# Bits of q placed right behind their signs and those of k behind its low rows; the overflow loop ahead of the last expert's closing step

## The chip, the cores and the metric

The kernel runs on one core of a Trainium2 chip. The metric is the time of the whole program on the device, in microseconds (us), as a median over runs. PE is the matrix engine (PEld its weight loads), DVE, ACT and POOL are the vector, scalar and GpSimd engines, and SP is the engine whose queue issues most of the DMA transfers.

## The reference, cut to what matters

Three steps follow each other. The first is attention in which a query sees only keys of its own hash bucket; the other two are feed-forward layers, the last with eight experts.

```python
def _attn_ref(q, k, v, proj):            # 2 batches, 8 heads, 768 rows, 64 columns
    q_bits = (np.einsum('bhsd,dk->bhsk', q, proj) > 0)      # 6 bits a row
    k_bits = (np.einsum('bhsd,dk->bhsk', k, proj) > 0)
    mask = q_bucket[:, :, :, None] == k_bucket[:, :, None, :]
    scores = np.where(mask, scale * np.matmul(q, k.transpose(0, 1, 3, 2)), -1e9)
    ...                                   # softmax, times v
x = _moe_ref(x)                           # 1536 tokens, gated layer 512 -> 1536 -> 512
def _moe2_ref(x, w_skip, w_gate, w1, w2): # 8 experts, tokens with skip_score > 0 only
    for e in range(E):                    # every chosen token goes to its best expert
        h = np.maximum(xc[mask] @ w1[e], 0.0)
        y[mask] = gate_w[mask, None] * (h @ w2[e])
    out[do_compute] = xc + y
```

## The kernel before

**Attention.** Two heads make a pair; there are 8 pairs of 12 units, a unit being 128 query rows of one head. For a unit PE multiplies twice into the same bank (`qk`): `t1q` by `t1k` (L501, 128 rows of operand), then `t2q` by `t2k` (L503, 76 rows: 64 rows of data and 12 rows of bits). Rows 64 to 76 of the t2 operands hold the bits of q and of k with such signs and sizes that products of unlike buckets fall far below the others. DVE takes the peak (L516), ACT the exponential (L530), POOL divides (L522 to L525), PE transposes (L539), and PE multiplies by v (L560).

While pair p-1 is computed, `prep(p)` makes the operands of pair p in the other half of the tile `RG`. Its steps: `cast` (ACT, L449) rounds k and q of one head to the short float type; `low` (DVE, L456) makes what the rounding left, over all 128 partitions of operand 3, so it also writes the rows where the bits of k will lie; `q_rows` (two DMAs, L460) copies q's rounded rows to operands 0 and 1; `k_rows` (one DMA, L463) copies k's within operand 2, over the rows that `q_rows` reads; `ql_rows` (one DMA, L466) copies q's low rows out of operand 3; `bits` (PE, L475) and `signs` (DVE, L478) make the bits in one tile; `place` (eight DMAs, L485) carries them to their rows: for each of two heads and two halves of the sequence one DMA for q (c = 0, operand 1) and one for k (c = 1, operand 3, over rows that `ql_rows` reads). A DMA row `RG<-RG 64x2x768` is 384 KB, one of `place` (`12x384`) 18 KB.

Where a step stands is set by the table `PLAN`: each step has a number in thousandths of a unit, all steps of attention are sorted by it (`at`, and the last lines of `attention`), and each engine takes its instructions in that order. SP's queue is in order: an instruction that waits holds up all behind it. Besides the copies above it carries for each pair the load of k and q of pair p+2 (`load`, L383, 768 KB), the load of v (L391), and on the way two pieces of the next layer's weights of 512 KB (`cv_load`, L226: `SS<-in_wg`, `in_wv`, `in_wo`), which POOL takes first (`cv_rebias`, L229).

**The end.** In `moe2` each expert ends with `deliver` (PE, the second product, L1118 to L1122) and `finish` (DVE, L1126, then a scatter to `out` that POOL issues, L1037). Experts with over 128 tokens are served by a loop behind all this (`over_tile` under `tc.For_i`, L1295 to L1298). Its count `n` is zero with these inputs; every engine still reads `n` (L1296) and takes the way around the body (L1297): it posts its semaphore for the skipped body once its own work is done, POOL waits for all scatters and posts theirs (`INC_SWDGE_SEM`), then every engine waits through a list of 12 semaphore waits, among them those on the scatters and on PE, and goes on to the program's end (L1386), where all engines meet twice.

Of the kernel before, what the change touches and what calls it, by code (L numbers as in the profile page):

```python
# [35 lines left out]
    "low0": 3769,  # L36
    "cast1": 444,
    "low1": 4884,
    "q_rows": 4912,
    "k_rows": 5120,  # L40
    "ql_rows": 6549,
    "place": 9379,
    "load": 16702,
    "bits": 1375,
    "signs": 1759,
# [12 lines left out]
    "first": (585, 787),  # L58
    "others": (2972, 1965, 2133, 3661),
    "warms": ((787, 3), (2467, 3), (2734, 3)),  # L60
}


# [4 lines left out]
def tile_kernel(  # L68
# [17 lines left out]
    nc = tc.nc  # L86
    NPAIR, D2, _, S = kq.shape
# [32 lines left out]
    def f32(ap):  # L120
        return ap.bitcast(F32)
# [252 lines left out]
    def bt_t(p):  # L374
        return rg(16 * S, S)
# [56 lines left out]
    def prep(p):  # L432

        def both(kind, rows):
            o = (p % 2) * 8 * S + kind * S
            return f32(RG[rows, o : o + 8 * S].rearrange("p (j x) -> p j x", j=2)[:, :, 0:S])

        up, dn = slice(0, D), slice(D, 2 * D)  # L440

        def cast(j):
            if PLAN["low"][j] == "P":
                PTS(raw_kq(p, j), raw_kq(p, j), kqs, 1.0, ALU.mult, ALU.mult)
                COPY[PLAN["cast"][j]](out=t_op(p, j, 2), in_=raw_kq(p, j))
            elif PLAN["cast"][j] == "V":
                TS(t_op(p, j, 2), raw_kq(p, j), kqs, None, ALU.mult)
            else:
                nc.scalar.mul(t_op(p, j, 2), raw_kq(p, j), kqs)  # L449

        def low(j):
            o = rg((p % 2) * 8 * S + (j * 4 + 3) * S, S)
            if PLAN["low"][j] == "P":
                PTT(out=o, in0=raw_kq(p, j), in1=f32(t_op(p, j, 2)), op=ALU.subtract)
            else:
                STT(out=o, in0=raw_kq(p, j), scalar=kqs, in1=f32(t_op(p, j, 2)), op0=ALU.mult, op1=ALU.subtract)  # L456

        def q_rows():
            for kind in (0, 1):
                dma(out=both(kind, up), in_=both(2, dn))  # L460

        def k_rows():
            dma(out=both(2, dn), in_=both(2, up))  # L463

        def ql_rows():
            dma(out=both(0, dn), in_=both(3, dn))  # L466

        st = {}

        def bits():  # L470

            st["b"] = psH()
            for t in range(4):
                j, h = divmod(t, 2)
                mm(st["b"][32 * t : 32 * t + 32, 0:HS], lhsT=padg, rhs=raw_kq(p, j)[:, h * HS : (h + 1) * HS], start=True, stop=True)  # L475

        def signs():
            TS(bt_t(p)[:, 0:HS], st["b"][:, 0:HS], thr[:, 0:1], thr[:, 1:2], ALU.is_gt, ALU.mult)  # L478

        def place():  # L480
            for t in range(4):
                j, h = divmod(t, 2)
                for c in range(2):
                    o = 32 * t + 16 * c
                    dma(out=f32(t_op(p, j, 1 + 2 * c)[D:T2R, h * HS : (h + 1) * HS]), in_=f32(bt_t(p)[o : o + 2 * NB, 0:HS]))  # L485

        return cast, low, q_rows, k_rows, ql_rows, bits, signs, place

# [169 lines left out]
    def attention():  # L658
        start_up()
        for u in range(NU):  # L660
            for name, f in (("qk", qk), ("exp", expo), ("tr", back), ("stats", stats)):
                at(1000 * u + PLAN[name][u % 4], f, u)
            for hf in range(2):
                at(1000 * u + PLAN["copy"][u % 4][hf], emptied, u, hf)
        for u in range(0, NU, 2):
            at(1000 * u + PLAN["scales"][u // 2 % 2], scales, u)
        for g in range(NU // 4):
            av_steps(g)
        for p in range(1, NPAIR):
            cast, low, q_rows, k_rows, ql_rows, bits, signs, place = prep(p)  # L670
            o = (p - 1) * PER * 1000 + (PLAN["late"] if p == 1 else 0)

            def put(name, f, *a):
                at(o + PLAN[name], f, *a)

            for j in range(2):
                put(f"cast{j}", cast, j)
                put(f"low{j}", low, j)
            put("q_rows", q_rows)
            put("k_rows", k_rows)  # L680
            put("ql_rows", ql_rows)
            put("bits", bits)
            put("signs", signs)
            put("place", place)
            if p + 2 < NPAIR:
                put("load", load, p + 2)
            at((p - 1) * PER * 1000 + PLAN["v"], load_v, p)
        for x in range(12):
            for y, f in enumerate((cv_load, cv_rebias, cv_shift, cv_low, cv_sign)):
                at(max(6000 * x + PLAN["cv"][y], PLAN["others"][2] + 1), f, x)  # L690
        for x in range(12, 15):
            at(1000 * (NU - 9) + 500, cv_load, x)
        xn = xnorm(0)
        sq, ad, me, fl, sp_, dg, sd, sc, hi_, lo_ = PLAN["xn"]
        for x in range(2):
            at(sq[x], xn["square"], x)
        for x in range(3):
            at(ad[x], xn["add"], x)
        at(me, lambda: xn["mean"](psH()))
        at(fl, xn["flat"])  # L700
        at(sp_, xn["spill"])
        for z in range(2 * TPB):
            at(dg[z // 2], xn["diag"], z)
        at(sd, lambda: xn["spread"](psH()))
        for k in range(NK):
            at(sc[k], xn["scale"], k)
            at(hi_[k], xn["high"], k)
            at(lo_[k], xn["low"], k)
        for x_, f, *a in PLAN["splits"]:
            at(1000 * NU + x_, split_gv if f else split_o, *a)  # L710
        for x_, z in PLAN["ahead"]:
            at(1000 * NU + x_, gate_products, 0, 0, z)
        for _, _, f, a in sorted(cal, key=lambda z: z[:2]):
            f(*a)
# [414 lines left out]
    def moe2(rt):  # L1129
        spl = {}  # L1130
        done = [0]
        state = {}
        over = iter(())

        def prep():
            n = done[0]
            if n < len(SEQ):
                spl[SEQ[n]] = split2(n, wch[n % 9])
                fetch(n + 9)
            done[0] += 1  # L1140
            if n > 6:
                next(over, None)

        for n in range(2):
            spl[SEQ[n]] = early.pop(n)
            done[0] += 1
        r = rt["finish"]()
        over = over_tables(r, state)
        xgs = [xyt[e // TPB][:, e % TPB] for e in range(NE)]
        for e in range(NE):  # L1150
            gather(xgs[e], r["idx"][:, e : e + 1])
            if e == 2:

                for n in range(6, 11):
                    nc.gpsimd.memset(wch[n % 9][0:1, 0, 0:1], 0.0)
                    fetch(n)
        r["rest"]()
        xo = {0: x_ops(0, xgs[0], True)}
        pu = {0: psA()}
        hs = {}  # L1160
        up(pu[0], xo[0], spl.pop((0, 0)), 0)
        prep()
        xo[1] = x_ops(1, xgs[1])
        prep()
        up(pu[0], xo[0], spl.pop((0, 1)), 1)
        hs[0] = relu(0, pu[0])
        r["rest_pe"]()
        prep()
        for e in range(NE):
            nx = e + 1 if e + 1 < NE else None  # L1170
            if nx:
                pu[nx] = psA()
                up(pu[nx], xo[nx], spl.pop((nx, 0)), 0)
            ht = turn(hs.pop(e))
            if nx:
                prep()
                up(pu[nx], xo[nx], spl.pop((nx, 1)), 1)
                hs[nx] = relu(nx, pu[nx])
                prep()
                if nx + 1 < NE:  # L1180
                    xo[nx + 1] = x_ops(nx + 1, xgs[nx + 1])
            ps = bank(6 + e % 2)
            for hf in range(2):
                deliver(ps, ht, spl.pop((e, 2 + hf)), hf)
                if hf:
                    finish(e, ps, xgs[e], r["gate"][:, e : e + 1], r["idx"][:, e : e + 1])
                prep()
        for _ in over:
            pass
        return r, state  # L1190


    def over_tables(r, state):
# [46 lines left out]
    def over_tile(op_, r, o):  # L1240
        cur = op_.tile([P, NTT], F32, name="cur")
        TS(cur, o["j"].broadcast_to([P, NTT]), -float(P), None, ALU.mult)
        TT(out=cur, in0=cur, in1=o["place"], op=ALU.add)
        slots = bank(7)
        for i in range(NTT):
            on = rg(14336 + (i % 2) * P, P)
            TS(on, iot, cur[:, i : i + 1], None, ALU.is_equal)
# [39 lines left out]
            deliver(ps, ht, split2(hf, spl[2 + hf]), hf)  # L1287
        finish(0, ps, xg, gt[:, 0:1], idx[:, 0:1])

    with tc.manual_schedule():  # L1290
        rt = routing()
        attention()
        moe1(rt)
        r, o = moe2(rt)
        with tc.tile_pool(name="op", bufs=1) as op_:  # L1295
            n = nc.values_load(o["n"][0:1, 0:1], min_val=0, max_val=NTT - 1)  # L1296
            with tc.For_i(0, n, 1):  # L1297
                over_tile(op_, r, o)  # L1298


def _limits(w):
# [88 lines left out]
```

## Time and profile before

| | us |
|---|---|
| median of 3 runs | 663.14 (662.63 to 665.33) |
| the profiled execution | 663.67 |
| its span, first to last instruction | 661.9 |
| PE busy | 642.7 (97%) |
| DVE, ACT, POOL busy | 531.0, 400.6, 279.2 |

Some 1.8 us of the profiled execution lie outside the span. Attention fills the span up to about 240 us, the first feed-forward layer runs to about 550 us, the experts to 653 us. Idle time is read engine by engine: a row of the timeline gives start, duration, engine, line, operation and tiles, and in brackets how long the engine had been idle and what ended it.

### The profile page before, as it was taken

The page shows a single profiled execution, that of the slowest core. Times are in us where ns is not written, and L with a number is a line of the kernel's source. Part 1 is how long each engine was busy: PE and PEld are TensorE (multiplying, and loading weights), DVE is VectorE, ACT ScalarE, POOL GpSimd, SP SyncE. Part 2 cuts the span into 40 slices and gives each one's busy share as a digit, 9 for nine tenths or more (in the row PEclk, how much of TensorE's full clock was granted, in tenths as well). Part 3 has the DMA queues.
Part 4 walks back from the last instruction along what each step waited for, and adds up shares of the span by engine and source line. Part 5 has one row for each costly group of instructions (what it writes and reads, how often), then busy time and mean ns, then how long its engine had stood idle before and what let it go on. Part 6 is the DMA issues. An engine that isn't in the chain of part 4 may idle for free. (4 is left out here: it accounts for less than half of the span.)

```text
span 661.9 us, 10521 instructions
## 1 busy us (share of the span) xinstructions
PE 642.7 (97%) x3596; PEld 508.8 (77%) x3596; DVE 531.0 (80%) x902; ACT 400.6 (61%) x725; POOL 279.2 (42%) x329
## 2 busy tenths in 40 slices
PE   7899999899999999999999999999999999999994
PEld 5567777677777768887888888888888888888883
DVE  5778888789897829998966786799999376999992
ACT  2778888789889846554444433344334344888880
POOL 3566666667976622455431215431113315111211
PEclk8899999999999999999999999999999999999998
DMA  7546536455344113453121000002404016999910
GB/s 232 133 114 170 166 95 195 143 131 160 92 101 144 66 33 128 160 162 125 59 84 63 2 1 0 1 0 94 164 16 177 0 64 207 386 390 389 386 60 26
DMA packets 43783, 84.72 MB, mean 128 GB/s; under 512 B 3506, under 2 KB 17106, under 8 KB 43600
## 3 DMA queue, kind: packets, MB, share of 16 engines
q1 hardware_dynamic: 42144, 80.62, 37.8%
q0 software_dynamic: 1280, 3.11, 1.3%
q8 instruction: 29, 0.48, 0.3%
q10 hardware_dynamic: 304, 0.30, 0.2%
q14 instruction: 26, 0.21, 0.1%
HBM read 67.55 MB, written 5.24 MB: 110 GB/s over the span
## 5 line engine op out<-in xcount | busy, mean ns | idle before, releaser
L306 POOL TENSOR_TENSOR RG<-WW,RG 128x512 fp32r<-128x512 f32 x35 | 64.9, 1855 | 184.1 <-ACT RG L305 176.4
L333 PE MATMUL PS<-RG 128*128 128x512 f32 x288 | 112.5, 391 | 0.0
L334 PE MATMUL PS<-RG 128*128 128x512 f32 x288 | 112.1, 389 | 0.0
L335 PE MATMUL PS<-RG 128*128 128x512 f32 x288 | 112.1, 389 | 0.0
L516 DVE TENSOR_REDUCE peak<-PS 128x1 f32<-128x768 f32 x96 | 91.6, 954 | 24.3 <-PE PS L503 18.7
L530 ACT ACTIVATE WW<-PS,shape 128x768 f32<-128x768 f32 x96 | 95.3, 998 | 21.2 <-DVE shape L517 20.0
L525 POOL TENSOR_SCALAR WW<-WW,rsum 128x768 f32<-128x768 f32 x96 | 86.5, 913 | 4.8
L732 ACT CAST RG<-BB 128x512 fp32r<-128x512 f32 x36 | 22.4, 622 | 107.2 <-DVE BB L730 107.2
L539 PE MATMUL PS<-cst,WW 128*128 128x128 f32 x576 | 81.4, 277 | 1.0 <-POOL WW L525 1.0
L539 PEld LDWEIGHTS PS<-cst,WW 128*128 128x128 f32 x576 | 63.9, 140 | 22.1 <-POOL WW L525 11.7
L1066 DVE TENSOR_TENSOR RG<-WW,RG 128x1024 fp32r<-128x1024 f32 x64 | 75.2, 1218 | 6.0 <-ACT RG L1064 5.8
L306 DVE TENSOR_TENSOR RG<-WW,RG 128x512 fp32r<-128x512 f32 x73 | 60.8, 871 | 8.3 <-ACT RG L305 8.3
L305 ACT CAST RG<-WW 128x512 fp32r<-128x512 f32 x108 | 61.5, 619 | 8.2 <-PE PS L750 4.2
L1064 ACT CAST RG<-WW 128x1024 fp32r<-128x1024 f32 x64 | 63.9, 1051 | 1.2 <-PE PS L1122 0.9
L333 PEld LDWEIGHTS PS<-RG 128*128 128x128 f32 x288 | 54.1, 188 | 11.8 <-issue 0.8
L335 PEld LDWEIGHTS PS<-RG 128*128 128x128 f32 x288 | 54.1, 188 | 11.3
L334 PEld LDWEIGHTS PS<-RG 128*128 128x128 f32 x288 | 54.1, 188 | 11.1
L501 PE MATMUL PS<-RG 128*128 128x512 f32 x192 | 56.4, 375 | 3.4 <-DVE RG L418 2.8
L748 PE MATMUL PS<-RG 128*128 128x512 f32 x144 | 56.5, 392 | 0.0
L750 PE MATMUL PS<-RG 128*128 128x512 f32 x144 | 56.3, 391 | 0.1
L749 PE MATMUL PS<-RG 128*128 128x512 f32 x144 | 56.1, 389 | 0.0
L503 PE MATMUL PS<-RG 76*128 76x512 f32 x192 | 50.8, 346 | 3.6 <-DMA RG<-RG 2.0
(192 smaller groups left out, 1264.7 us busy)
## 6 DMA issues: line engine op xcount, KB each, us to landing
WW<-in_w SPq DMA_DIRECT2D x32, 1024.0 KB
RG<-RG SPq DMA_DIRECT2D x28, 384.0 KB
WW<-in_kq SPq DMA_DIRECT2D x7, 768.0 KB
SS<-in_wo SPq DMA_DIRECT2D x9, 512.0 KB
SS<-in_wg SPq DMA_DIRECT2D x8, 512.0 KB
SS<-in_wv SPq DMA_DIRECT2D x8, 512.0 KB
WW<-in_v SPq DMA_DIRECT2D x8, 384.0 KB
XY<-in_wg SPq DMA_DIRECT2D x4, 512.0 KB
```

The lines of the kernel that those rows point to most:

```text
L305: copyA(out=hi, in_=src)
L306: sub(out=lo, in0=src, in1=f32(hi), op=ALU.subtract)
L333: mm(o, lhsT=h[:, k], rhs=xpart(b, 0, k), start=(k == 0), stop=False)
L334: mm(o, lhsT=h[:, k], rhs=xpart(b, 1, k), start=False, stop=False)
L335: mm(o, lhsT=l[:, k], rhs=xpart(b, 0, k), start=False, stop=(k == NK - 1))
L516: red(out=a[:, 1:2], in_=u_st[u][:, 0:S], axis=AX.X, op=ALU.max, negate=True)
L525: PTS(e_t(x), e_t(x), rsum[:, x % NS : x % NS + 1], 1.0, ALU.mult, ALU.mult)
L530: nc.scalar.activation(out=e_t(u), in_=s[:, 0:S], func=AF.Exp, bias=c, scale=b, accum_out=sums[:, u % NS : u % NS + 1])
L539: nc.tensor.transpose(ps[:, x * P : (x + 1) * P], e_t(u)[:, kt * P : (kt + 1) * P], ident)
L748: mm(acc[t], lhsT=hh[:, sl], rhs=oh, start=(f == 0), stop=False)
L1064: copyA(out=hi[:, sl], in_=src[:, sl])
L1066: f(out=lo[:, sl], in0=src[:, sl], in1=f32(hi[:, sl]), op=ALU.subtract)
```

## The change

Four numbers of `PLAN` change and one is added, so that `prep`'s steps stand in another order; `place` is called once for q and once for k. The loop over the overflow moves into `moe2`, between the last `deliver` and the last `finish`, and takes another bank for its slots.

```diff
-    "q_rows": 4912,
-    "k_rows": 5120,
-    "ql_rows": 6549,
-    "place": 9379,
+    "q_rows": 3500,
+    "k_rows": 4920,
+    "ql_rows": 4900,
+    "place": 3000,
...
+    "place2": 6000,
...
-        def place():
+        def place(c):
             for t in range(4):
                 j, h = divmod(t, 2)
-                for c in range(2):
-                    o = 32 * t + 16 * c
-                    dma(out=f32(t_op(p, j, 1 + 2 * c)[D:T2R, h * HS : (h + 1) * HS]), in_=f32(bt_t(p)[o : o + 2 * NB, 0:HS]))
+                o = 32 * t + 16 * c
+                dma(out=f32(t_op(p, j, 1 + 2 * c)[D:T2R, h * HS : (h + 1) * HS]), in_=f32(bt_t(p)[o : o + 2 * NB, 0:HS]))
...
-            put("place", place)
+            put("place", place, 0)
+            put("place2", place, 1)
...
                 if hf:
+                    if not nx:
+                        for _ in over:
+                            pass
+                        overflow(r, state)
                     finish(e, ps, xgs[e], r["gate"][:, e : e + 1], r["idx"][:, e : e + 1])
                 prep()
-        for _ in over:
-            pass
-        return r, state
...
-        slots = bank(7)
+        slots = bank(6)
...
+    def overflow(r, o):
+        with tc.tile_pool(name="op", bufs=1) as op_:
+            n = nc.values_load(o["n"][0:1, 0:1], min_val=0, max_val=NTT - 1)
+            with tc.For_i(0, n, 1):
+                over_tile(op_, r, o)
+
     with tc.manual_schedule():
         rt = routing()
         attention()
         moe1(rt)
-        r, o = moe2(rt)
-        with tc.tile_pool(name="op", bufs=1) as op_:
-            n = nc.values_load(o["n"][0:1, 0:1], min_val=0, max_val=NTT - 1)
-            with tc.For_i(0, n, 1):
-                over_tile(op_, r, o)
+        moe2(rt)
```

What it does to the order is seen first on SP's queue, during `prep(4)`. Before (L383 load, L460 q_rows, L463 k_rows, L226 a piece of weights, L466 ql_rows, L485 place, L391 load of v):

```order
L383 DMA WW<-in_kq 128x1536
L460 DMA RG<-RG 64x2x768 x2
L463 DMA RG<-RG 64x2x768
L226 DMA SS<-in_wv 128x4x256
L466 DMA RG<-RG 64x2x768
L485 DMA RG<-RG 12x384 x8
L391 DMA WW<-in_v 128x768
L226 DMA SS<-in_wo 128x1024
```

Now, in the same place of SP's queue (lines are shifted by one: L461 q_rows, L384 load, L467 ql_rows, L464 k_rows, L227 the piece, L485 place):

```order
L485 DMA RG<-RG 12x384 x4
L461 DMA RG<-RG 64x2x768 x2
L384 DMA WW<-in_kq 128x1536
L467 DMA RG<-RG 64x2x768
L464 DMA RG<-RG 64x2x768
L227 DMA SS<-in_wv 128x4x256
L485 DMA RG<-RG 12x384 x4
L392 DMA WW<-in_v 128x768
L227 DMA SS<-in_wo 128x1024
```

Four of the eight copies of bits moved ahead of q_rows, the load moved behind q_rows, ql_rows moved ahead of k_rows and of the piece of weights, and the other four copies stand behind that piece as all eight did. The order on PE, ACT and, within attention, on DVE and POOL is as it was.

The second place is DVE's end of the program. Before, the last closing step stands ahead of the reading of the loop's count:

```order
L1110 TENSOR_TENSOR RG<-PS,RG 128x512 x2
L1126 SCALAR_TENSOR_TENSOR SS<-PS,gt,XY 128x512
L1296 TENSOR_LOAD n_over
L1297 COMPARE_AND_BRANCH
L1297 UNCONDITIONAL_BRANCH x2
```

Now, on DVE, from the same step to the program's end, the loop's body left out:

```order
L1111 TENSOR_TENSOR RG<-PS,RG 128x512 x2
L1294 TENSOR_LOAD n_over
L1295 COMPARE_AND_BRANCH
L1295 UNCONDITIONAL_BRANCH x2
...
L1295 UNCONDITIONAL_BRANCH
L1127 SCALAR_TENSOR_TENSOR SS<-PS,gt,XY 128x512
L1390 UNCONDITIONAL_BRANCH
```

The closing step moved behind the loop and its branches, and so does POOL's last scatter (L1038), which stands behind `L1295 UNCONDITIONAL_BRANCH` on POOL's queue; behind the scatter the program's end begins, where SP waits for its landing.

## Rows read from the trace of the kernel before

**Rows 1.** The page, busy time of each engine, share of the span, instructions.

```profile
PE 642.7 (97%) x3596; PEld 508.8 (77%) x3596; DVE 531.0 (80%) x902; ACT 400.6 (61%) x725; POOL 279.2 (42%) x329
```

**Rows 2.** Waits of PE, 20 to 240 us: total, times, longest.

```profile
PE PS L503 <- DMA RG<-RG: 2.0, 2, 1.9
PE PS L503 <- issue: 1.3, 1, 1.3
```

**Rows 3.** Timeline of PE where a pair begins: start, duration, work, idle before.

```profile
45.16 0.59 PE L503 MATMUL PS<-RG 76*128 76x512 f32 x2 [1.29 <-issue]
...
72.80 0.85 PE L475 MATMUL PS<-WW,padg 128*32 128x384 f32 x8
...
99.46 0.85 PE L475 MATMUL PS<-WW,padg 128*32 128x384 f32 x8
...
127.69 0.61 PE L503 MATMUL PS<-RG 76*128 76x512 f32 x2 [1.85 <-DMA RG<-RG]
128.23 0.85 PE L475 MATMUL PS<-WW,padg 128*32 128x384 f32 x8
```

**Rows 4.** Timeline of SP's queue, 100 to 128 us, preparation of pair 4.

```profile
104.05 1.40 SPq L460 DMA_DIRECT2D RG<-RG  x2
111.21 0.59 SPq L463 DMA_DIRECT2D RG<-RG  x1
111.89 0.55 SPq L226 DMA_DIRECT2D SS<-in_wv  x1
112.49 1.38 SPq L466 DMA_DIRECT2D RG<-RG  x1
113.92 11.82 SPq L485 DMA_DIRECT2D RG<-RG  x8
```

**Rows 5.** Waits of SP's queue, 100 to 128 us.

```profile
SPq L485 <- DMA RG<-RG: 5.6, 1, 5.6
```

**Rows 6.** Timeline of DVE in the same preparation: signs, and the second low.

```profile
101.10 0.67 DVE L478 TENSOR_SCALAR RG<-PS,cst 128x384 fp32r<-128x384 f32 x1
...
110.17 1.01 DVE L456 SCALAR_TENSOR_TENSOR RG<-WW,kqs,RG 128x768 fp32r<-128x768 f32 x1
```

**Rows 7.** Timeline of POOL, preparations of pairs 3 and 4, at a piece of weights.

```profile
92.10 0.65 POOL L229 TENSOR_SCALAR SS<-SS 128x512 f32<-128x512 f32 x1
93.51 0.19 POOL L522 TENSOR_SCALAR rsum<-sums 128x2 f32<-128x2 f32 x1 [0.75 <-ACT WW L530]
...
119.71 0.66 POOL L229 TENSOR_SCALAR SS<-SS 128x512 f32<-128x512 f32 x1 [0.92 <-DMA SS<-in_wv]
```

**Rows 8.** Stretches: length, engines' busy time, PE's clock, DMA share, GB/s at the end.

```profile
113.00:114.00 1.00, 1.00 (x11) 0.62 (x11) 1.00 (x2) 0.98 (x3) 1.00 (x2) 1.00 0.98 206
115.00:116.00 1.00, 1.00 (x9) 0.92 (x8) 0.56 (x1) 1.00 (x3) 0.08 (x1) 1.00 0.99 310
```

**Rows 9.** Timelines of PE, DVE and POOL at the end of the program.

```profile
652.16 1.07 PE L1122 MATMUL PS<-RG 128*128 128x512 f32 x4
...
653.27 0.75 DVE L1126 SCALAR_TENSOR_TENSOR SS<-PS,gt,XY 128x512 f32<-128x512 f32 x1 [3.83 <-PE PS L1122]
...
648.51 0.98 POOL L1037 DMA_INDIRECT out<-SS,sidx  x1 [9.98 <-DVE SS L1126]
654.29 0.99 POOL L1037 DMA_INDIRECT out<-SS,sidx  x1 [4.79 <-DVEq L1297]
```

**Rows 10.** Issue to landing of the last scatter (L1037, from 654.2 us).

```profile
DMA to landing us min/median/max: 3.0/3.0/3.0
```

**Rows 11.** The loop's line on POOL's queue from 656 us: durations in ns, starts.

```profile
L1297 POOLq INC_SWDGE_SEM  x1: 500/500/500, 657.4 to 657.4; - x1
...
L1297 POOLq EVENT_SEMAPHORE  x12: 42/43/43, 658.4 to 659.4; - x12
```

**Rows 12.** The program's end on POOL's queue, 659 to 661 us.

```profile
L1386 POOLq DRAIN  x1: 1387/1387/1387, 659.6 to 659.6; - x1
```

**Rows 13.** The loop's line on PE's queue, 649 to 654 us.

```profile
L1297 PEldq EVENT_SEMAPHORE  x1: 51/51/51, 653.3 to 653.3; - x1
```

**Rows 14.** The page, a queue that fetches instructions: packets, MB, share of 16 engines.

```profile
q8 instruction: 29, 0.48, 0.3%
```

## The prediction

> **What bounds the kernel now.** I read the page first: PE is busy for 97% of the span [rows 1], and no other engine above 80%. A change here gains time only where it closes one of PE's gaps or shortens what follows PE's last multiplication. So the second view is PE's waits in attention. Two entries touch the line L503, whose right operand holds the bits of k: 2.0 us put down to a DMA within the core, and 1.3 us put down to "issue" [rows 2]. The timeline places them [rows 3]: 1.29 us at 45.16, where pair 1 begins, and 1.85 us at 127.69, where pair 4 begins; the rest of the 2.0 us, about 0.2, belongs to a third pair. What such a gap costs in all is seen by the distance of the small products L475, one group a pair: 26.66 us from 72.80 to 99.46, where nothing waits, and 28.77 from 99.46 to 128.23. The pair with a gap of 1.85 us is 2.11 us longer, so it isn't caught up later: two products that else overlap are parted too, for 0.26 us more.
>
> Why the bits are late is seen on SP's queue [rows 4]. The eight copies start at 113.92, but the second, the first one of k, waits for the landing of ql_rows for 5.6 us [rows 5], because it overwrites rows that ql_rows reads. The last copy has been issued at 125.74, some seven copies later. The four copies of q wait for nothing of the kind; they stand behind k's only by the order.
>
> The third view is the end. PE's last product ends at 653.23 [rows 9], and the span at 661.9: 8.7 us with PE idle.
>
> **The change part by part.**
>
> *Four copies fewer behind ql_rows.* The queue needs (125.74 - 113.92 - 0.8 - 5.6) / 7 = 0.75 us for each copy [rows 4, 5]. Now three issues and a landing follow the landing of ql_rows, in place of six and a landing, as q's first copy had gone ahead: at least three times 0.75 = 2.3 us sooner. The largest wait to be closed is 1.85 us. In addition ql_rows leaves sooner: it waited behind k_rows and a piece of weights until 112.49, while the low rows that it needs were there at 111.18 [rows 6], and 384 + 512 KB were ahead of it in the transfers. At 206 GB/s for copies within the core and 310 GB/s for weights [rows 8] that is 1.9 + 1.7 us. Against it stands the load of 768 KB, which now comes after q_rows: 2.5 us at 310 GB/s. But q_rows leaves 7 us before ql_rows; its 768 KB take 3.8 us and the load's 2.5, so the load has just passed. I take it that ql_rows lands 3 to 5 us sooner, and the bits of k 5 to 7. All three gaps close: 1.29 + 1.85 + 0.2 = 3.3 us by the gaps, and up to 4.1 with 0.26 for each. I take 3.8.
>
> *Four copies ahead of q_rows.* Signs end at 101.77 [rows 6], so four copies hold SP until 104.8, and q_rows, which left at 104.05, goes 0.7 us later. Who waits for it is k_rows, whose other condition (the low rows at 111.18) comes later; the slack is over 1 us, and the price nothing. If q_rows slipped by 2 us, k_rows would follow, with 10 us left to the next pair.
>
> *The piece of weights behind ql_rows.* This has a price. The piece that left at 111.89 now goes behind ql_rows too and arrives 1.9 us later. POOL takes it in order between its divisions, for which PE's transposes wait. In the preparation of pair 4 it was late before: POOL waited 0.92 us [rows 7], and PE shows no other gap there than the one at 127.69. In that of pair 3 POOL had 0.75 us of idle time right behind the piece [rows 7]. So POOL can lose some 0.9 us for nothing, and what is more falls on PE. By the rates, a piece landed 1 to 2 us before POOL asked for it, in the preparations of pairs 2, 3, 5 and 6; 1.9 us more makes a wait of 0 to 1 us there, which the slack nearly covers, and some 0 to 1.5 beyond it in that of pair 4. I take 0.5 us in all, between 0 and 2.5.
>
> *The loop ahead of the last closing step.* Before, the end is one chain: closing step 653.27 to 654.02, scatter from 654.29 [rows 9], landing 3.0 us later at 657.3 [rows 10]; POOL's posting of the scatters' semaphores 657.4 to 657.9, a jump of 0.5 us, its 12 waits to 659.4 [rows 11], another jump of 0.2, a drain of 1.39 us to 661.0 [rows 12], and 0.9 us in which the engines meet. Now the loop's way around needs only the scatter of expert 6 (issued at 648.51 [rows 9], so landed before 652) and PE's end. Posting, jumps and all waits but the last pass while PE still multiplies. PE posts its end at 653.3 [rows 13]; DVE passes its last wait and jumps, 0.05 + 0.2 us, and the closing step begins at 653.6, 0.35 later than before. Then 0.75 us of it, 0.27 to the scatter, 3.0 to the landing: 657.65. SP, which waits for that, and the meeting take 0.2 + 0.9 us: 658.75, a gain of 3.15 us. The drain is hidden if it starts when POOL reaches it, at 655.9, as it did before within 0.2 us of the last jump: it ends at 657.3, ahead of the landing. This row is the nearest that there is. Where POOL's drain must first see the landing, 1.2 us come back and the gain is 1.95. With a landing of 2.6 us, as an upper bound, it is 3.5. I take 3.2.
>
> A rule of the Trainium skill speaks against this part: by "Runtime: NRT & Kernel Launch", section "Instruction fetch mechanics", a taken branch whose target lies outside the two pages held on the engine stalls until that page has been fetched. Its result is the second rival below.
>
> *The sum.* 3.8 - 0.5 + 3.2 = 6.5 us. From the profiled execution, 663.67, that is 657.2. The median lies 0.5 us below that execution, so 656.6. The bounds of the terms, 4.1 - 0 + 3.5 and 3.3 - 2.5 + 1.95, give gains of 7.6 and 2.8: 655.5 and 660.4. The other edit, bank 6 in place of 7 in the loop's body, costs nothing, since the body doesn't run.
>
> **The rivals.**
>
> *The weights come too late, and it is slower.* The mechanism is the one above: load, ql_rows and k_rows ahead of the piece, POOL waiting for it in five pairs, PE for POOL. Beyond the 0.9 us of slack each pair pays in full. If the load hadn't passed and its 2.5 us stood ahead too, the piece would be 4.4 us later, less a margin of 1 to 2, that is 2.4 to 3.4 late, and 1.5 to 2.5 us a pair would fall on PE: 7.5 to 12.5 us against a gain of 7.0, so 663.6 to 668.6. It decides from 1.4 us a pair on. For it speaks the wait of 0.92 us; against it that the load has room to pass, and that POOL is busy for 42% [rows 1]. Partial cases of it give 658 to 661.
>
> *Jumps cost a fetch.* The code behind the loop is now on the path. The queue that fetches for an engine moved 29 blocks in 0.3% of 16 engines' span [rows 14], about 1.1 us each. One such fetch on DVE and one on POOL would give back 2.2 us: 658.8. The jumps in the trace, 0.2 and 0.5 us, speak against it [rows 11, 12], and that the engines stand at the page of the last jump some 1.5 us before PE ends. By the page named above it would come so if the block behind the loop lies in a page not yet held; no run here shows that.
>
> *The change doesn't do what it says.* If ql_rows lands no sooner and the copies wait for the transfers ahead of them, the gaps stay open, and the end's gain is all: 3.2 less 0.5, 660.5.
>
> **How the numbers follow.** The forecast (both gains, 655.3 to 658.5): 0.64. Late weights in part, or a fetch, or the drain behind the landing (658.5 to 659.8): 0.20. Gaps that stay or several of these together (659.8 to 663): 0.11. Slower by late weights: 0.05, of which 0.04 beyond 0.5%. A measurement of this kernel tells about 0.5% from no change, 3.3 us. Faster by more: 0.84; within: 0.12; slower by more: 0.04. The range of 8 in 10 goes from 654.9, somewhat below the lower bound for the spread of the runs, to 660.4.
>
> **What would show it.** In the profile of the changed kernel L503 has no idle time behind a DMA where pairs begin, and the distance of L475 is 26.7 us from pair 2 to 5. POOL's rows at the pieces of weights show waits of 0 to 1 us, and PE's waits for the divisions (L525) don't grow. The last closing step starts 0.3 to 0.5 us behind PE's last product, the last scatter lands 3 us after its issue, and the span ends 5.0 to 5.8 us behind PE in place of 8.7. The prediction is wrong if POOL waits over 1 us at each odd piece with PE idle behind it, if POOL's drain starts only at the landing, or if DVE stands over 1 us between PE's end and the closing step.

## The result, and the profile after

The changed kernel takes 657.24 us (median of 6 runs, 654.78 to 658.04), the kernel before 664.11 in the same measurements. The ratio is 0.989, with a 95% interval from 0.9865 to 0.9915: some 7.3 us less, between 5.6 and 9.0 (6.9 by the medians). The forecast was 656.6, within 654.9 to 660.4, and a gain of 6.5 us, counted from the 663.14 of the first three runs.

The profiled execution took 657.49 us with a span of 655.5, against 663.67 and 661.9. The first row of the page, which answers to [rows 1], shows the same work in a shorter span:

```profile
PE 643.1 (98%) x3596; PEld 510.3 (78%) x3596; DVE 530.0 (81%) x902; ACT 400.9 (61%) x725; POOL 279.1 (43%) x329
```

Waits of PE from 20 to 240 us (total, times, longest), to be laid beside [rows 2]. The two entries of L503 are gone, and these are all that is left:

```profile
PE PS L539 <- POOL WW L525: 1.0, 2, 0.7
PE PS L501 <- ACT WW L530: 0.6, 1, 0.6
```

PE's timeline at the small products of the bits, one group a pair, beside [rows 3] (lines are shifted by one):

```profile
23.68 0.85 PE L476 MATMUL PS<-WW,padg 128*32 128x384 f32 x8
...
45.13 0.85 PE L476 MATMUL PS<-WW,padg 128*32 128x384 f32 x8
...
71.79 0.85 PE L476 MATMUL PS<-WW,padg 128*32 128x384 f32 x8
...
98.45 0.85 PE L476 MATMUL PS<-WW,padg 128*32 128x384 f32 x8
```

From the second group on the distance is 26.66 us, and the next groups, at 125.11 and 151.77, keep it; only the last distance is longer, 27.97 us (28.18 before). Before, the groups stood at 22.53, 45.68, 72.80, 99.46 and 128.23. So 1.70 us came out between the first and the second, 0.46 between the second and the third, 2.11 between the fourth and the fifth. The first group, however, is 1.15 us **later** than before, which the two parts of the change don't explain; that comes back below.

SP's queue in the preparation of pair 4, beside [rows 4] (L461 q_rows, L384 load, L467 ql_rows, L464 k_rows, L227 the piece of weights, L485 the bits):

```profile
100.79 3.18 SPq L485 DMA_DIRECT2D RG<-RG  x4
104.06 1.38 SPq L461 DMA_DIRECT2D RG<-RG  x2
105.49 1.18 SPq L384 DMA_DIRECT2D WW<-in_kq  x1
110.20 0.60 SPq L467 DMA_DIRECT2D RG<-RG  x1
110.90 0.59 SPq L464 DMA_DIRECT2D RG<-RG  x1
111.59 1.36 SPq L227 DMA_DIRECT2D SS<-in_wv  x1
114.35 3.15 SPq L485 DMA_DIRECT2D RG<-RG  x4
```

The four copies for k start at 114.35, right behind the landing of ql_rows, and are issued by 117.50. Counted from the pair's group of small products, that first copy goes 15.9 us into the pair in place of 21.0 (120.43 before), and the last one is out at 19.1 in place of 26.3. By the trace the last bits land at 118.89, and PE takes them at 124.67.

POOL at the pieces of weights, beside [rows 7]:

```profile
92.29 0.65 POOL L230 TENSOR_SCALAR SS<-SS 128x512 f32<-128x512 f32 x1 [1.18 <-DMA SS<-in_wo]
...
118.92 0.65 POOL L230 TENSOR_SCALAR SS<-SS 128x512 f32<-128x512 f32 x1 [1.14 <-DMA SS<-in_wv]
```

It now waits for an odd piece in five of the preparations, for 0.75 to 1.18 us (for the two shortest of these waits the row names a step of DVE, which ends within 0.1 us of the piece's landing), and PE's waits for the divisions stayed at 1.0 us in all. From the end of the division behind the piece to PE's transposes of that unit 0.25 and 0.30 us are left in these two places, and 0.66 where POOL waits 0.75 and 0.77. In the preparation of pair 1, where it waits 0.96, only 0.06 are left, and PE stands idle for 0.06.

The end of the program, beside [rows 9], [rows 10] and [rows 12]: PE's last products, the closing step on DVE, the last two scatters on POOL, then issue to landing of the last scatter, and the drain on POOL's queue (shortest, middle and longest of three, in ns, then first and last start):

```profile
648.78 1.07 PE L1123 MATMUL PS<-RG 128*128 128x512 f32 x4
...
650.24 0.75 DVE L1127 SCALAR_TENSOR_TENSOR SS<-PS,gt,XY 128x512 f32<-128x512 f32 x1 [4.18 <-PEq L1295]
...
645.14 0.99 POOL L1038 DMA_INDIRECT out<-SS,sidx  x1 [9.98 <-DVE SS L1127]
651.26 0.98 POOL L1038 DMA_INDIRECT out<-SS,sidx  x1 [5.14 <-DVE SS L1127]
...
DMA to landing us min/median/max: 2.7/2.7/2.7
...
L1390 POOLq DRAIN  x3: 40/109/3625, 651.0 to 655.2; - x3
```

PE ends at 649.85. The closing step starts 0.39 us later, the scatter 1.02 us behind that, it lands at 653.95, and the span ends at 655.50: 5.65 us behind PE in place of 8.63.

### The profile page after: what moved, and what is told of

It reads as the page before. It is cut to its first block, busy times and chain, and to the rows that moved or that the text cites. A ratio compares the mean times of both kernels' runs of the same rounds, so it can differ in the third digit from the quotient of the medians.

```text
span 655.5 us, 10531 instructions
## 1 busy us (share of the span) xinstructions
PE 643.1 (98%) x3596; PEld 510.3 (78%) x3596; DVE 530.0 (81%) x902; ACT 400.9 (61%) x725; POOL 279.1 (43%) x329
## 5 line engine op out<-in xcount | busy, mean ns | idle before, releaser
L885 DVE CUSTOM_DVE_ANT_0 EX<-XY,SS 128x512 f32<-128x512 f32 x64 | 50.1, 782 | 1.6
```

## The experiments

The unit of all comparisons is the kernel before, which ran on the same chip beside each set. Where a kernel ran only once, it is judged by its rows first; its time alone is uncertain by some 1.5 us either way, as the six runs of the changed kernel lie 3.3 us apart.

**The two parts apart.** The new order of the preparation with the old end, and the reverse:

```diff
 # e1_plan_only, against the changed kernel
                 if hf:
-                    if not nx:
-                        for _ in over:
-                            pass
-                        overflow(r, state)
...
+        for _ in over:
+            pass
+        return r, state
...
-        moe2(rt)
+        r, o = moe2(rt)
+        with tc.tile_pool(name="op", bufs=1) as op_:
+            n = nc.values_load(o["n"][0:1, 0:1], min_val=0, max_val=NTT - 1)
+            with tc.For_i(0, n, 1):
+                over_tile(op_, r, o)
 # e2_end_only, against the changed kernel
-    "q_rows": 3500, "k_rows": 4920, "ql_rows": 4900, "place": 3000, "place2": 6000,
+    "q_rows": 4912, "k_rows": 5120, "ql_rows": 6549, "place": 9379,
...
-            put("place", place, 0)
-            put("place2", place, 1)
+            put("place", place)
```

> The new order of the preparation alone, the end of the program as it was. Theory (the two parts add): PE has no gap at L503 where pairs begin, the distance of the small products of the bits is 26.7 us in every pair, and against the kernel before this is worth 1.42 + 0.36 + 2.11 us up to the fourth pair and 4.1 us in all, counted from the first pair on; PE's last product to the span's end stays 8.6 us. Time 660.0 (664.1 less 4.1), with 1 us either way from how long PE's clock stays at its lower level in the first 25 us. Rival (most of the 7 us comes from the end): no more than 2 us faster, 662.

> The loop ahead of the last closing step alone, the preparation's order as before. Theory: the gaps of 1.3, 0.2 and 1.9 us at L503 stay, and the span ends 5.6 us behind PE's last product in place of 8.6: 3.0 us faster, 661.1. POOL's drain ends 0.7 us behind the landing of the last scatter, as in the changed kernel (654.65 against 653.95); if it only needs 1.4 us from its start, as in the kernel before, it ends ahead of the landing and the gain is 3.6. Rival (the end's gain needs the other part): less than 1.5 us.

Measured: the preparation alone 660.41 us, ratio 0.9932 (0.9915 to 0.995), 4.5 us less (4.3 by the medians); the end alone 661.54 us, ratio 0.9955 (0.9935 to 0.9974), 3.0 us less. The product of the two ratios is 0.9887, and the whole change has 0.989: the parts add. In the preparation alone the distance of the small products is 26.66 us from the second pair on (27.97 for the last), as expected, but one gap is left where pair 1 begins (PE's timeline):

```profile
43.97 0.59 PE L503 MATMUL PS<-RG 76*128 76x512 f32 x2 [0.86 <-DMA RG<-RG]
```

The expectation of no gap anywhere was wrong there: pair 1 is prepared amid the start of the program and has less room than the others. The changed kernel has the same order and no gap there in its profile, so this gap comes and goes with the time at which PE arrives. In the end alone the gaps at these products (L504 there) stay (1.29, 0.48 and 1.80 us), and the span ends 5.66 us behind PE. Its drain ends 0.71 us behind the landing, as in the changed kernel.

**Which part of the new order.** q's four copies alone, and the order of the large copies alone, both with the old end (both also have the other bank in the loop's body, which doesn't run):

```diff
 # e3_q_bits_only, against the kernel before
-    "place": 9379,
+    "place": 3000,
+    "place2": 9379,
...
-            put("place", place)
+            put("place", place, 0)
+            put("place2", place, 1)
 # e4_rows_only, against the kernel before
-    "q_rows": 4912, "k_rows": 5120, "ql_rows": 6549,
+    "q_rows": 3500, "k_rows": 4920, "ql_rows": 4900,
```

> Only q's four copies of bits moved ahead of q_rows; load, q_rows, k_rows, piece of weights, ql_rows and k's copies in the order of before; the end as before. Theory (the queue's share alone, three copies fewer behind the landing of ql_rows, 2.3 us): k's last bits land 2.3 us sooner, 0.5 us ahead of PE's need in the worst pair, and no gap over 0.1 us is left: time as with the whole new order, 660. Rival (q's copies push q_rows, and with it ql_rows, back by 0.7 us or more): gaps of 0.2 to 1 us stay in two pairs, 661 to 662.

> Only the order of the large copies: load behind q_rows, ql_rows ahead of k_rows and of the piece of weights; all eight copies of bits together behind the piece as before; the end as before. Theory (ql_rows lands 5 us sooner, and that alone is more than the largest gap): last bits land 5 us sooner, no gap is left, 660. If it were only the queue's order that counts and the landing moved with the transfers ahead, gaps of over 1 us stay, 662 to 663.

The large copies alone came as expected but for pair 1: 661.11 us, all distances but the last 26.66 us from the second pair on, and one gap of 1.4 us at pair 1. q's copies alone were a surprise: 668.24 us, **slower** than the kernel before (664.67). Waits of PE in that kernel, 20 to 240 us:

```profile
PE PS L539 <- POOL WW L525: 3.2, 3, 1.3
PE PS L503 <- DMA RG<-RG: 2.8, 2, 2.2
...
```

SP's queue in the same kernel, preparation of pair 4, says why:

```profile
107.02 3.13 SPq L485 DMA_DIRECT2D RG<-RG  x4
110.19 0.51 SPq L384 DMA_DIRECT2D WW<-in_kq  x1
110.81 1.38 SPq L461 DMA_DIRECT2D RG<-RG  x2
119.01 0.59 SPq L464 DMA_DIRECT2D RG<-RG  x1
119.70 0.94 SPq L227 DMA_DIRECT2D SS<-in_wv  x1
```

In the kernel before, the load (now L384) left at 98.68, 5.4 us ahead of q_rows. Behind q's copies, which wait for the signs, it leaves 5.5 us into the pair and 0.6 us ahead of q_rows. k_rows waits for q_rows' landing and leaves at 14.3 us in place of 11.75, the piece behind it follows, and ql_rows behind that leaves at 16.0 in place of 13.0. My expectation had counted copies on the queue and not the load that the same edit moved.

**The load's place.** So the load was moved by itself: in the losing kernel behind q_rows, and in the changed kernel ahead of q_rows.

```diff
 # e8_q_bits_load, against e3_q_bits_only
-    "load": 16702,
+    "load": 16914,
 # e9_load_ahead, against the changed kernel
-    "load": 16702,
+    "load": 15400,
```

> The run with only q's copies of bits moved, which came out at 668, with one thing more: the load of the next k and q stands behind q_rows, as in the changed kernel; k_rows, the piece, ql_rows and k's copies stay where they were before; the end as before. Theory (that run lost because the load came to stand between q's copies and q_rows and its 768 KB went ahead of them): q_rows lands near 10 us into the pair, ql_rows lands as in the kernel before, near 21, k's last bits near 26, and from the second pair on no gap over 0.2 us is left; time 660 to 661.5. Rival (q's copies themselves hold up the queue too long): the gaps behind POOL's divisions in the third and fifth pair stay, 666 to 668.

> The changed kernel with the load put ahead of q_rows, behind q's copies of bits; all else as changed. Theory (the load's place decides over the weights): q_rows lands 3 us later, k_rows waits for it and leaves 3 us later, the piece behind it lands 1 to 2 us later, POOL waits 2 to 3 us for it, and PE loses 0.5 to 1.5 us in each of four or five pairs; bits of k still in time: 660 to 663. Rival (in the new order ql_rows no longer waits behind k_rows, so the load's place doesn't count): 657.

With the load behind q_rows the four distances from the second pair on are 26.66 us, as the theory had it: the gaps of pairs 2 to 5 are gone with one number. The time, 663.77 us, missed the expected 660 to 661.5, since pair 1 got worse: its gap is 2.2 us, and its distance 26.06 in place of 23.15 before. That is 2.9 us more, where the gap is 0.9 longer; behind the gap PE's granted clock stands at the lower of its two levels, 1.2 GHz in place of 2.4, from 45.0 to 48.4 us, and the kernel with q's copies alone has the same gap and the same fall, from 45.9 to 49.3. Pair 1 has no load to be moved, and its piece of weights still stands ahead of ql_rows. From the first group of small products to the last, the load's place makes 4.9 us between these two kernels.

The reverse cost the changed kernel what was expected: 662.03 us. Waits of PE in it, 20 to 240 us:

```profile
PE PS L539 <- POOL WW L525: 3.9, 4, 2.4
...
```

On its SP queue ql_rows leaves as soon as in the changed kernel, 11.75 us into the pair, but k_rows 3.6 us behind it in place of 0.7, and the piece 0.7 us behind that. POOL waits 4.20, 1.48, 1.83 and 2.24 us for four odd pieces; where it waits 4.20, PE loses 2.44, where 2.24, PE loses 0.50, and at the other two PE stands for 0.05.

The wait of 2.44 us costs more than itself, for PE's granted clock falls behind it, from 72.7 to 76.1 us (length, PE's busy time and matmuls, granted clock, DMA share, GB/s):

```profile
72.00:74.00 2.00, 2.00 (x12) 0.67 0.00 0
74.00:76.00 2.00, 2.00 (x12) 0.50 0.00 0
```

The two distances around it are 30.31 and 27.22 us, 4.2 over 26.66 and so 1.8 more than the wait. A part of the 4.8 us that this run lies above the changed kernel is the clock, then, and not the weights.

**How late may the weights be?** The odd pieces were put behind k's bits, and, the other way, ahead of ql_rows:

```diff
 # e5_piece_last: + 10, e6_piece_first: - 1100; against the changed kernel
-    at(max(6000 * x + PLAN["cv"][y], ...), f, x)
+    at(max(6000 * x + PLAN["cv"][y] + (10 if y == 0 and x % 2 else 0), ...), f, x)
```

> The changed kernel with the odd pieces of weights behind k's four copies of bits in place of ahead of them, so that they leave some 6 us later and arrive 2.5 to 3 us later. Theory (POOL's slack is what keeps the weights' lateness off PE, and in the changed kernel only 0.25 to 0.30 us of it is left in two of the preparations): POOL waits 3.6 to 4 us for each of five odd pieces, and PE waits for the divisions for 2 to 2.5 us in each of these pairs: 667 to 669. Rival (the pieces are off the path): POOL waits as long, PE doesn't, 657.

> The changed kernel with the odd pieces of weights ahead of ql_rows in place of behind k_rows. Theory (weights and bits are both in time in the changed kernel, the one with 0.25 us, the other with over 5 us to spare): the pieces land 2 us sooner, POOL waits for them for less than 0.3 us in all but the first, ql_rows and k's bits come 2 us later and still 3 us early; no gap of PE changes, and the time is that of the changed kernel, 657, 1.5 us either way from the clock at the start. Rival (POOL's waits of 0.8 to 1.2 us cost PE something that the gaps don't show): 2 us faster.

Late pieces: 670.53 us, a little over the expected 667 to 669. Waits of PE from 20 to 240 us, and three of the five places in PE's timeline:

```profile
PE PS L539 <- POOL WW L525: 12.7, 7, 3.3
...
```

```profile
70.51 0.87 PE L539 MATMUL PS<-cst,WW 128*128 128x128 f32 x6 [1.88 <-POOL WW L525]
...
100.52 1.54 PE L539 MATMUL PS<-cst,WW 128*128 128x128 f32 x6 [3.29 <-POOL WW L525]
...
130.57 0.87 PE L539 MATMUL PS<-cst,WW 128*128 128x128 f32 x6 [1.80 <-POOL WW L525]
```

POOL waited 3.62, 5.07 and 3.54 us ahead of these three: 1.74 to 1.78 us of each wait cost PE nothing, the rest all of it. The two waits of the kernel with the load ahead give the same, 1.76 and 1.74. That is the slack of a piece this late, and the changed kernel uses 1.2 us of it. By its own rows only 0.20 to 0.25 us are left there and not 0.55, since 0.05 us lie between the division and the transposes even where PE waits. The rest of the difference stands in POOL's first step behind the piece, in the changed kernel and in this one:

```profile
93.03 0.51 POOL L522 TENSOR_SCALAR rsum<-sums 128x2 f32<-128x2 f32 x1
...
98.48 0.19 POOL L522 TENSOR_SCALAR rsum<-sums 128x2 f32<-128x2 f32 x1
```

That the time came out above the expected goes with PE's clock again: behind the wait of 3.29 us it stands at 1.2 GHz from 100.4 to 103.8 us, and that pair's distance is 4.9 us over 26.66. Behind the waits of 2.44 and 2.34 us in the two later pairs it didn't fall.

Early pieces: POOL's only wait for weights is that for the first (3.8 us), k's bits still land 4.5 us ahead of PE's use, and the distances from the second pair on are again 26.66 us but for the last. 656.39 us in one run isn't told apart from 657.24; as expected, nothing was to be had there.

**What the drain waits for.** The last scatter was replaced by a plain transfer to the first rows of the output, so that the last expert's rows stay unwritten:

```diff
 # e11_no_last_scatter, against the changed kernel, in finish
-        scatter(ix, o)
+        if e == NE - 1:
+            dma(out=out[0:P], in_=o)
+        else:
+            scatter(ix, o)
```

> The changed kernel without the last scatter: the last expert's tile is written by a plain transfer on SP's queue to the first 128 rows of the output, so the last expert's rows stay unwritten. It asks what POOL's drain at the program's end waits for; with the scatter it ended 0.70 us behind the landing in two kernels. Theory (it waits for the scatter's own landing): with no scatter outstanding it takes 1.4 us from its start, as in the kernel before, ends ahead of the plain transfer's landing, and the span ends 0.9 to 1.0 us behind that landing in place of 1.55. Rival (the drain lasts 3.6 us of itself when it starts there, or ends 0.7 us behind any last transfer): the span ends 1.5 us behind the landing as before.

POOL's queue at the program's end in that kernel (as in the last row of the changed kernel above):

```profile
L1393 POOLq DRAIN  x3: 40/103/1305, 650.3 to 654.3; - x3
```

The drain takes 1.3 us, from 650.3, and is over before the plain transfer lands at 653.62; the span ends at 654.58, 0.96 us behind that landing. With the scatter the drain starts at 651.03, ahead of the scatter, and takes 3.63 us, to 0.71 us behind the landing, and the span ends 1.55 us behind it. So it waits for the scatter of its own engine, and by the difference of 1.55 and 0.96 that costs 0.6 us of the end.

**The start of the program.** The stretches of 2 us at the start (length, PE's busy time and matmuls, granted clock, DMA share, GB/s), first of the kernel before, then of the changed one:

```profile
8.00:10.00 2.00, 0.25 (x2) 1.00 0.83 255
10.00:12.00 2.00, 0.98 (x3) 0.72 0.84 270
12.00:14.00 2.00, 2.00 (x8) 0.50 0.81 281
...
20.00:22.00 2.00, 2.00 (x13) 0.72 0.32 83
22.00:24.00 2.00, 2.00 (x20) 1.00 0.99 310
```

```profile
8.00:10.00 2.00, 0.67 (x3) 0.94 0.83 209
10.00:12.00 2.00, 0.81 (x3) 0.50 0.95 301
...
20.00:22.00 2.00, 2.00 (x10) 0.50 0.25 60
22.00:24.00 2.00, 2.00 (x13) 0.65 0.97 304
```

PE stands idle for 2.4 to 2.8 us ahead of attention's first product, within 8.1 to 11.2 us, and its clock falls to the lower of its two levels, 1.2 GHz. It came back at 21.1 us in the profile of before and at 23.4 in that of after. Over the eleven profiles with this idle time the low stretch lasted 10.2 us in six and 13.7 us in five, with one and the same start-up code. Is it the idle time? Eleven small products of ones, the kind that start-up has already (`keep_warm`), were put there:

```diff
 # e7_fill, against the changed kernel, at the end of the start-up's products
+        keep_warm(11, 3)
```

> The changed kernel with eleven more small products of ones ahead of the first product of attention, where PE stands idle for 2.5 us from 8.7 to 11.2 us. In the profiles PE's clock falls to 1.2 GHz at 10 to 11 us, and comes back at 21 to 23.2 us; where it came back 2 us later the first pair was over 0.7 us later. Theory (the fall follows from this idle time, and the length of the low stretch is what moves the time from run to run): the granted clock stays 1.00 from 4 to 24 us, the first pair ends 2 to 4 us sooner, 653.5 to 655.5, and the runs lie closer together than the 3.3 us of the changed kernel's. Rival (the clock falls all the same, or VectorE and ScalarE set the pace there): under 0.5 us, 657.

The clock stays up (the same stretches of this kernel):

```profile
8.00:10.00 2.00, 2.00 (x17) 1.00 0.87 205
10.00:12.00 2.00, 2.00 (x17) 1.00 0.95 326
...
22.00:24.00 2.00, 1.72 (x13) 1.00 0.10 24
```

The time is 655.52 us (654.25 to 657.05), ratio 0.9874 (0.9853 to 0.9896). That is 1.7 us below the changed kernel's median (1.1 by the two ratios), at the upper edge of the 653.5 to 655.5 expected, and the runs lie 2.8 us apart, hardly closer than the 3.3 of the changed kernel: the low stretch isn't all that moves them. PE reached the bits of pair 1 at 40.85 us in place of 44.6, and there part of it went to a new gap:

```profile
42.37 0.58 PE L503 MATMUL PS<-RG 76*128 76x512 f32 x2 [1.52 <-DMA RG<-RG]
```

This is pair 1 again. Its piece of weights goes ahead of ql_rows, because `late` moves only the preparation. So that one piece was put ahead of q's bits:

```diff
 # e10_fill_piece1, against e7_fill
-    at(max(6000 * x + PLAN["cv"][y], ...), f, x)
+    at(max(6000 * x + PLAN["cv"][y] - (1996 if x == 1 and y == 0 else 0), ...), f, x)
```

> The changed kernel with the eleven products of ones, and the second piece of weights (the first odd one) on SP's queue ahead of q's bits of pair 1, where before it stood between q_rows and ql_rows. With the ones alone PE reached pair 1 at 40.85 us and waited 1.52 us there for k's last bits (0.27 more for the copies of pair 0's end), as ql_rows landed only at 36.24 behind that piece. Theory (the piece's 512 KB stood ahead of ql_rows): ql_rows lands 1.5 to 2 us sooner, the gap closes to under 0.3 us, POOL no longer waits for that piece, and the time is 1.2 to 1.8 us less than with the ones alone: 654.0, which is also the fastest kernel here. Rival (the low rows or PE's own order set ql_rows, not the piece): gap as before, 655.5.

SP's queue in the preparation of pair 1, with the ones alone (L467 ql_rows, then the second L485, k's bits), and with the piece moved:

```profile
26.40 1.21 SPq L227 DMA_DIRECT2D SS<-in_wv  x1
27.71 1.84 SPq L467 DMA_DIRECT2D RG<-RG  x1
...
36.25 3.15 SPq L485 DMA_DIRECT2D RG<-RG  x4
```

```profile
19.15 0.59 SPq L227 DMA_DIRECT2D SS<-in_wv  x1
...
26.75 1.12 SPq L467 DMA_DIRECT2D RG<-RG  x1
...
32.97 3.16 SPq L485 DMA_DIRECT2D RG<-RG  x4
```

k's bits go 3.3 us sooner, and of PE's waits for bits in pair 1 none is left (the one wait at L503, 0.7 us at 21.6, belongs to pair 0). The time is 653.6 us (652.72 to 656.3), ratio 0.9861 (0.9836 to 0.9885): the fastest kernel of this study by its median and its profile (span 650.8). The intervals of the three last kernels overlap, so the runs alone don't part it from the changed kernel; the rows do.

## Why the prediction was right, step by step

**The gaps of the bits: right, somewhat better than said.** The gaps of [rows 3] are closed, and the distances show 1.70, 0.46 and 2.11 us for the three of them, 4.3 in place of 3.8. "0.26 more than the gap" was read from the third; the second bears it out (0.46 for a gap of 0.20), the first, amid the start, has 0.41 more. The first is also the least sure: with the same order of the preparation pair 1 has a gap of 0.86 us in the preparation alone, 0.31 without the last scatter and 1.52 with the ones, so that its closing in the changed kernel hangs on when PE arrives. ql_rows was to land 3 to 5 us sooner and landed 5.1 us sooner within its pair; the bits were to land 5 to 7 us sooner and landed 7.7 sooner. Of the two reasons that I gave, fewer copies behind ql_rows and a sooner ql_rows, the second alone closes every gap but that of pair 1. The first alone, which brings the load ahead of q_rows, loses 3.6 us in its one run; with the load behind q_rows it too closes the gaps of pairs 2 to 5. I had told of the load only that it "has just passed" when ql_rows leaves. By the trace it hadn't quite: in the preparation of pair 4 the load lands at 111.84, 1.6 us behind ql_rows' issue. ql_rows was quick even so, 4.1 us from its issue to its landing in place of 7.9. What the sign hung on was the load's place behind q_rows: ahead of it, it takes back 4.8 us in its run, about all that this part gains.

**The price of the late weights: the mechanism right, the size too high.** I took 0.5 us, between 0 and 2.5, on a slack of 0.9 us. POOL did come to wait 0.75 to 1.18 us at the pieces, within the 0 to 1.5 of the prediction, and PE lost 0.06 us in the preparation of pair 1 and else nothing that shows, as the slack is 1.4 us by the changed kernel's rows and 1.75 for a later piece. I had read 0.9 from POOL's waits and its idle time behind one piece, 0.75 us [rows 7]. That is only a part: in the same rows 0.66 us lie between the end of the division and PE's transposes, 0.61 of which can be spent. The 0.4 us that are left to 1.75 lie in POOL's two short steps behind the piece, 0.89 us behind a late one in place of 1.33 (L522 and L523: 0.19 and 0.70 against 0.19 and 1.14).

**The slower rival** had its mechanism and its place right, which the late pieces show in full (670.5 us, 12.7 us of PE behind POOL in place of 1.0), and decided later than I wrote: a piece has to come 1.4 to 1.75 us behind POOL's need before PE pays, and not 0.9.

**The end: right in sum, by two errors that nearly cancel.** PE's end to the closing step took 0.39 us (0.37 by the prediction), the way to the scatter was as said, and the landing 2.7 us in place of 3.0. What follows the landing took 1.55 us in place of 1.1, because POOL's drain isn't hidden: the alternative that I had named, that it must first see the landing, is what happens. But then it needs 0.71 us more and not 1.39, so it gives back 0.6 us of the 1.2. In sum 2.98 us of the 3.15.

**Jumps that fetch code: no.** The changed kernel's page has the same row as [rows 14], 29 packets, 0.48 MB; and DVE's step starts 0.2 us behind its jump (650.03 to 650.24), as the jumps before the change took. The page "Runtime: NRT & Kernel Launch" of the Trainium skill, section "Instruction fetch mechanics", lets a jump stall where its target isn't held; here no such stall shows, and whether the target was held no run tells.

**What no step had: the start.** In these two profiles PE came 1.15 us later to its first group of small products, as its clock came back 2.3 us later. The profiles alone don't tell whether that is the run or the change: the long stretch of 13.7 us stands in five of the seven kernels with the new order of the large copies, and in none of the four with the old order. For the run speaks that the granted clock over the whole span differs among the runs of one kernel: 0.989 to 0.994 in the six of the changed kernel (0.989 in the profiled one, 0.994 in the fastest, 654.78 us) and 0.984 to 0.992 in the ten of the end alone. At 0.994 some 8 us at 1.2 GHz are left in all (an estimate: twice 0.006 of 652.8 us), less than in any of the eleven profiles. So the length changes with the run; whether the order has a part in it too stays open. PE's ends lie 3.38 us apart (653.23 and 649.85); with the 1.15 us that is 4.5 us for attention, which is what the preparation alone measured. The sum, then: 4.5 for the gaps in place of 3.8, nearly nothing lost for the weights in place of 0.5, and 3.0 for the end in place of 3.2. The single terms were off by up to 0.7 us, in both directions.

## What to carry to other kernels

When a step is moved on a queue in order, look at every transfer that it comes to stand ahead of or behind, not only at its own: here the place of one load of 768 KB, which an edit moves as a side effect, was worth 4.5 and 4.8 us in two pairs of runs, in the second partly through PE's clock. An engine's lateness is to be priced by all that lies on the way to the first use of its result: its own idle time and the time from its result to that use. Either alone was too little here. At a program's end, put what doesn't depend on the last result ahead of it, and count the drain of the engine that issues the last scatter behind that scatter's landing.

## What the runs showed of the hardware

POOL's drain at the end of the program takes 1.3 to 1.4 us where no scatter is outstanding, and with one it ends 0.71 us behind the landing, in two kernels alike. An idle time of PE of 2.4 to 2.8 us at the start was followed in eleven profiles by 10.2 us (six) or 13.7 us (five) at 1.2 GHz, while PE was busy nearly all of that time; filled with eleven products of ones, the clock stayed at 2.4 GHz in both profiles. That took only 1.7 us off the median, as PE then waits for others: it is busy for 0.89 us of the two from 20 to 22 us. Inside attention waits of PE of 2.2 us (in two kernels), 2.4 and 3.3 us were each followed by a stretch at 1.2 GHz, and two of 2.3 and 2.4 us were not.
